# Sparse attention and a ReGLU feed-forward on one core: feed-forward banks, V products and attention pieces placed anew

## The chip, the cores and the metric

The kernel runs on one core of a Trainium2 chip. The metric is the device time of one execution in microseconds (us), the median of several runs. The engines are TensorE (PE, with its weight loads as PEld), VectorE (DVE), ScalarE (ACT), GpSimd (POOL) and SyncE (SP), which here issues DMAs only. Each engine works through its own instructions in the order in which the program has them.

## The reference

Two stages follow each other. The first is attention over q, k and v of shape (4, 8, 768, 64): 4 batches, 8 heads, 768 rows. A row sees the first 8 columns (global) and the 96 columns up to itself (local), with a bias that falls with the distance.

```python
scores = scale * np.matmul(q, k.transpose(0, 1, 3, 2))
keep = is_global | is_local
scores = scores + bias[None, :, :, :]          # -slope of the head * distance
scores = np.where(keep, scores, -1000000000.0)
a = np.exp(scores - max); a = a / sum(a)
attn = np.matmul(a, v)
```

The second is a feed-forward with a ReLU gate over x, the attention's output as 3072 rows of 512:

```python
gate = np.maximum(x @ w_gate, 0.0)             # 512 -> 1536
val = x @ w_val
out = gate * val @ w_out                       # 1536 -> 512
```

## The kernel before

The 3072 rows are worked in eight halves of 384 rows; half s is rows of batch s // 2. In the code they are counted from 0 (`s` in the attention, `c` in the feed-forward); this text counts them from one, so that half four is s = 3. The order of all work is written out by hand: a function that is called records its instructions on every engine at that place.

**Stages.** Stage one, on the PSUM pools `s` (two tiles of two banks) and `t` (four of one bank), does the attention of half one, a pair of heads p at a time, in small steps: `scores`, `masks`, `first_values` (V rows of the first half brought to their places by selector matmuls, then copied out of PSUM), `first_sums` (what = 0: sums of the weights; what = 1: product with V), `first_inverse` (Ln, then Exp of minus that, on ACT, into a tile `rc`) and `first_product` (DVE: product times inverse into `xT`, the feed-forward's input). Stage two, on pools `s`, `ff` and `t`, begins the feed-forward of half one (`begin`: for the first gate and the first val block, parts 0 to 2 of 4) and weaves it with the attention of half two. Pools take the eight PSUM banks in the order in which they are named; a tile waits for whoever used its bank in the stage before.

From the third stage on the pools are `ff` (3), `qk` (3) and `av` (2). `ffn_pieces(c)` gives the feed-forward of a half as items of about 0.65 us: 12 gate and 12 val blocks in turn (`gate` L518 with a ReLU on ACT, `val` L518 with a product `ht` on DVE), then output blocks. From half three on the output uses seven products of sums (L577), for which DVE makes `cb`, `ad` and `de` from `ht`; `behind` hangs these sums on val blocks 2, 5, 8, 9, 10 and 11. On val 11 hang three: ad, cb and de.

`attention_pieces(s)` gives the attention as a list of pieces: QK(p), three per head pair p (scores on PE L408, Exp on ACT L411, mask product on DVE L420), and AV(p), two per pair (product with V on PE L436, Ln on ACT L445; the second also the Exp L450 and two products into `xT` on DVE L453). Its end mixes pairs 2 and 3, where g is QK(3) and a is AV(2):

```python
return (QK(0) + QK(1) + AV(0) + QK(2) + AV(1) + g[0:1] + gap + a[0:1] + g[1:2] + a[1:2] + g[2:3]
        + gap + AV(3))
```

`spread(items, first, last)` puts the pieces at equal distances between two shares of the feed-forward's length, and `weave` records each piece behind the first item that reaches its share. While half c's feed-forward runs, the attention of half c + 1 is woven in. An empty piece (`gap`) takes a place and does nothing.

**Loads.** `early_pieces(s)` casts k and q on POOL (`kc`, `qz`), transposes them by DMA from SP's queue (`piece_xk` L376 into kN, `piece_xq` L380 into qT) and orders the keys on POOL (kT). Weights are loaded through POOL's queue; `wo_sb`, the output weights, is the last and largest, and a POOL instruction (`held`) waits for it before half three's last casts. Half four's q and k (`qs`, `ks`) are loaded behind half three's ordered keys. SP's queue carries in this order: three output stores of half one, half four's three kN transposes, another store, its three qT transposes, two more stores.

Of the kernel before, what the change touches and what calls it, by code (L numbers as in the profile page):

```python
# [8 lines left out]
FP32 = mybir.dt.float32  # L9
# [6 lines left out]
def kernel(  # L16
# [21 lines left out]
    HP = H // 2  # L38
    QH = S // 2
# [26 lines left out]
    rc_pool = ctx.enter_context(tc.tile_pool(name="rc", bufs=2))  # L66
# [6 lines left out]
    firstp = first.enter_context(tc.tile_pool(name="firstp", bufs=1, side="right"))  # L73
# [6 lines left out]
    def open_psum(**pools):  # L80
        stack = ExitStack()
        for name, bufs in pools.items():
            psum[name] = stack.enter_context(
                tc.tile_pool(name=name, bufs=bufs, space=PSUM, reuse_waits="tile"))
        return stack
# [35 lines left out]
    def v_dst(b, r0, r1, j):  # L121
        t = vbuf[b % 2][r0:r1, j, D:]
        return t.rearrange("p (h z) -> p h z", z=2 * D)[:, :, 0:D]
# [48 lines left out]

    v3 = firstp.tile([128, H, NN * D], BF16, name="v3")
    vb3 = firstp.tile([128, H, D], BF16, name="vb3")
    rc0 = [firstp.tile([128, QH], FP32, name=f"rc{p}") for p in range(3)]
    kq0 = firstp.tile([128, 2, H, NN * D], FP32, name="kq0")
    kq1 = setupp.tile([128, 2, H, NN * D], BF16, name="kq1")

# [131 lines left out]
    def first_values(j, copy):  # L310
        vt = psum["t"].tile([128, 512], FP32, name="t_ps")
        for n in range(NN):
            nc.tensor.matmul(vt, lhsT=sel[:, n, j, :], rhs=v3[:, :, n * D : (n + 1) * D],  # L313
                             start=(n == 0), stop=(n == NN - 1))
        copy(v_dst(0, 0, 128, j) if j < 3 else vb3, vt.rearrange("r (h d) -> r h d", d=D))
# [3 lines left out]
    def distances(p, g):  # L319
        ps = biased_of[p, g] = psum["s"].tile([128, 2, 512], FP32, name="s_ps")  # L320
        for e in range(2):
            c = 0
            for i, (j, a, w, m) in enumerate(by[0, j] for j in steps_of[0][g]):
                nc.tensor.matmul(ps[:, e, c : c + NN * w].rearrange("k (n t) -> k n t", n=NN),
                                 lhsT=diag[:, 2 * p + e],
                                 rhs=dd[:, 0 if j == 0 else 1, :, m : m + w],
                                 start=(i == 0), stop=False, skip_group_check=True)
                c += NN * w

    def scores(s, p, g):  # L330
        half = s % 2
        spans_ = [by[half, j] for j in steps_of[half][g]]
        biased = half == 0 and 2 * p < NB
        if biased and (p, g) not in biased_of:
            distances(p, g)
        ps = biased_of[p, g] if biased else psum["s"].tile([128, 2, 512], FP32, name="s_ps")
        es = ef_pool.tile([128, 2, 360], BF16, name=f"ef{g}")
        cols = sum(NN * w for _, _, w, _ in spans_)
        qd = qTb[s][:, p, 0, :].rearrange("d (n t) -> d n t", n=NN)
        c = 0  # L340
        for i, (j, a, w, m) in enumerate(spans_):
            for e in range(2):
                r = slice(64 * e, 64 * e + 64)
                nc.tensor.matmul(ps[:, e, c : c + NN * w].rearrange("k (n t) -> k n t", n=NN),  # L344
                                 lhsT=kT[0][p][r, j, :], rhs=qd[r, :, a : a + w],
                                 start=(i == 0 and not biased), stop=(i == len(spans_) - 1),
                                 skip_group_check=True)
            es_of[s, p, j] = (es, c)
            c += NN * w
        nc.scalar.activation(es[:, :, 0:cols], ps[:, :, 0:cols], AF.Exp, bias=0.0, scale=scale)  # L350
# [13 lines left out]
    def piece_cast_k(s, p):  # L364
        nc.gpsimd.tensor_copy(  # L365
            kc.rearrange("t n (h d) -> t h n d", d=D)[:, 2 * p : 2 * p + 2],
            ks_of[s][:, 2 * p : 2 * p + 2, :].rearrange("t e (n d) -> t e n d", n=NN))
# [7 lines left out]
    def piece_xk(s, n):  # L375
        nc.sync.dma_start_transpose(  # L376
            out=kNb[s % 2][:, :, n * 128 : (n + 1) * 128], in_=kc[:, n])
# [10 lines left out]
    def early_pieces(s):  # L388
        out = [(0.0, lambda p=p: piece_cast_k(s, p)) for p in range(HP)]
        out += [(0.0, lambda n=n: piece_xk(s, n)) for n in range(NN)]  # L390
        out += [(0.0, lambda p=p: piece_cast_q(s, p)) for p in range(HP)]
        out += [(0.0, lambda n=n: piece_xq(s, n)) for n in range(NN)]
        out += [(0.0, lambda p=p: piece_order(s, p)) for p in range(HP)]
        return out
# [61 lines left out]
    def first_sums(s, p, what, tile_=None):  # L456
        half = s % 2
        todo = [by[half, j] for g in steps_of[half] for j in g]
        av = psum["t"].tile([128, 512], FP32, name="t_ps") if tile_ is None else tile_[:, what]
        av3 = av[:, 0:QH].rearrange("d (n p) -> d n p", n=NN)  # L460
        for i, (j, a, w, m) in enumerate(todo):
            es, c = es_of[s, p, j]
            for e in range(2):
                z0 = D + 2 * D * (2 * p + e)
                vals = vb3[:, 2 * p + e] if (half, j) == (0, 3) else vbuf[0][:, j, z0 : z0 + D]
                nc.tensor.matmul(av3[64 * e : 64 * e + 64, :, a : a + w],
                                 lhsT=ones if what == 0 else vals,
                                 rhs=es[:, e, c : c + NN * w].rearrange("k (n p) -> k n p", n=NN),
                                 start=(i == 0), stop=(i == len(todo) - 1),
                                 skip_group_check=True)  # L470
        av_of[s, p, what] = av
# [6 lines left out]
    def first_inverse(s, p):  # L478
        ln = rc_pool.tile([128, QH], FP32, name="lnd")
        nc.scalar.activation(ln, av_of[s, p, 0][:, 0:QH], AF.Ln, bias=0.0, scale=1.0)  # L480
        rc = rc0[p % 3] if s == 0 else rc_pool.tile([128, QH], FP32, name="rcp")
        nc.scalar.activation(rc, ln, AF.Exp, bias=0.0, scale=-1.0)
        av_of[s, p, "r"] = rc

    def first_product(s, p):
        if s not in xT_of:
            xT_of[s] = xt_pool.tile([128, N_DC, QH], BF16, name="xT")
        nc.vector.tensor_tensor(xT_of[s][:, p, :], av_of[s, p, 1][:, 0:QH], av_of[s, p, "r"], op=ALU.mult)  # L488
# [2 lines left out]
        first_inverse(s, p)  # L491
        first_product(s, p)

    def attention_pieces(s):
        QK = lambda p: [(0.18, lambda g=g: piece_qk(s, p, g)) for g in range(3)]
        AV = lambda p: [(0.29, lambda e=e: piece_av(s, p, e)) for e in range(2)]
        g = QK(3)
        a = AV(2)
        gap = [(0.0, lambda: None)]
        return (QK(0) + QK(1) + AV(0) + QK(2) + AV(1) + g[0:1] + gap + a[0:1] + g[1:2] + a[1:2] + g[2:3]  # L500
                + gap + AV(3))

# [142 lines left out]
    def spread(items, first, last):  # L647

        n = len(items)
        return [(first + (i + 0.5) / n * (last - first), f) for i, (_, f) in enumerate(items)]  # L650
# [14 lines left out]
    V, A, P = nc.vector.tensor_copy, nc.scalar.copy, nc.gpsimd.tensor_copy  # L665
# [6 lines left out]
    stack = open_psum(s=2, t=4)  # L672
# [44 lines left out]
    first_keys(3, V)  # L717
    distances(2, 1)
    scores(0, 2, 0)
    first_values(0, V)  # L720
    scores(0, 2, 1)
    make_mask(5)
    first_values(1, V)
    scores(0, 3, 0)
    first_values(2, V)
    masks(0, 3, 0)
    scores(0, 3, 1)
    masks(0, 3, 1)
    first_values(3, A)
    spread_v_globals(0, 3, NT)  # L730
    first_sums(0, 2, 0)
    first_inverse(0, 2)
    first_sums(0, 0, 1)
    first_product(0, 0)
    first_sums(0, 3, 0)
    first_inverse(0, 3)
    for p in range(1, HP):
        first_sums(0, p, 1)
        first_product(0, p)
    stack.close()  # L740
# [3 lines left out]
    kc = pool.tile([128, NN, DM], BF16, name="kc")  # L744
    qz = pool.tile([128, NN, HP, 2, 128], BF16, name="qz")

    stack = open_psum(s=2, ff=2, t=2)
    f1_0, f2_0 = ffn_pieces(0)
    f1_1, f2_1 = ffn_pieces(1)
    g_of = [begin_of[0][1]] + [f for _, f in f1_0[2::2]]  # L750
# [57 lines left out]
    for f in (*cast_k[:3], *cast_q[:3], lambda: nc.gpsimd.tensor_copy(held, wo_sb[0:1, N_FC - 1, 0:1]),  # L808
# [4 lines left out]
    weave(f1_1[G[0]])  # L813
    weave(f1_1[G[1]], [(0.1 + 0.12 * j, lambda j=j: fill_ones(nc.vector, 0, j)) for j in range(NT)])
    weave(f1_0[G[2]] + f1_1[G[2]] + f2_0 + f2_1,
          spread(attention_pieces(2), 0.43, 0.92), spread(early_pieces(3), 0.6, 0.92),
          spread([(0.0, lambda name=name, part=part: wo_sum(name, part)) for name in late["bs"] for part in range(2)],
                 0.2, 0.8))

    for c in range(2, NHALF):  # L820
        placed = []
        if c + 1 < NHALF:
            placed.append(spread(attention_pieces(c + 1), 0.0, 0.78))
        if c + 2 < NHALF:
            load_qk(c + 2, 0, H)
            load_v_half(c + 2)
            placed.append(spread(early_pieces(c + 2), 0.25, 0.75))
        f1, f2 = ffn_pieces(c)
        weave(f1 + f2, *placed)
# [35 lines left out]
```

## Time and profile before

| What | Value |
|---|---|
| median of 3 runs | 244.82 us (244.53 to 245.05) |
| the profiled execution | 244.51 us |
| its span, first to last instruction | 242.6 us |
| granted TensorE clock | 1.000 |
| busy in the span | PE 97%, DVE 70%, ACT 63%, POOL 38% |
| DMA moved | 33.75 MB, 139 GB/s on the mean |

A row of the timeline gives the start in us from the span's start, the time it took, the engine, the line of the kernel, the operation, what it writes and reads, and how many instructions are in the row; in brackets, how long the engine was idle before it and what ended that. A row of the waits gives the engine, the line that waited, who ended the wait, and the total, number and longest of these waits in us. The chain of waits is followed back from the last instruction; its pieces have a start, a length and an engine, queue or DMA.

### The profile page before, as it was taken

To read this page: it belongs to the slowest core of one execution; us is meant where nothing else is said; L and a number is where in the kernel's file an instruction comes from. 1 tells how busy PE (TensorE), PEld (TensorE's weight loads), DVE (VectorE), ACT (ScalarE), POOL (GpSimd) and SP (SyncE) were. 2 spreads that over 40 slices of the span, in tenths; PEclk is the share of its full clock that TensorE was granted. 3 is DMA by queue.
4 is the path that set the end of the run, shared out by engine and by line. 5 is a ranking of instruction groups with operands and counts; after the bars stand their busy time and mean duration, and the time that the engine had idled before them with its cause. 6 is when DMAs were issued, how large, how long until landed. Compare 5 with 4: busy or idle time off the path is not lost.

```text
span 242.6 us, 5086 instructions
## 1 busy us (share of the span) xinstructions
PE 234.6 (97%) x1819; PEld 148.6 (61%) x1819; DVE 168.8 (70%) x442; ACT 152.3 (63%) x316; POOL 92.4 (38%) x233
## 2 busy tenths in 40 slices
PE   7899999999999899999999999999999999999994
PEld 3555555665554566586667666686667666685663
DVE  7775954756674478857796688858796678854643
ACT  5987883433885677647874687647874587634330
POOL 6866896119257436803555057302540000000000
PEclk9999999999999999999999999999999999999999
DMA  6999999997999999779459768829491200020003
GB/s 206 187 195 177 261 241 208 176 107 136 289 176 175 237 237 112 101 133 286 89 110 109 232 184 153 60 106 285 82 118 43 91 0 0 3 104 25 3 15 115
DMA packets 79392, 33.75 MB, mean 139 GB/s; under 512 B 56952, under 2 KB 76408, under 8 KB 79368
## 3 DMA queue, kind: packets, MB, share of 16 engines
q1 hardware_dynamic: 46408, 23.82, 41.7%
q0 software_dynamic: 31744, 8.71, 34.5%
q10 hardware_dynamic: 1216, 0.92, 1.2%
q8 instruction: 14, 0.23, 0.4%
q14 instruction: 10, 0.08, 0.1%
HBM read 28.41 MB, written 6.29 MB: 143 GB/s over the span
## 4 chain that ended last, share of the span: by engine, by line
PE 67%; DMA 19%; POOL 4%; DVE 3%; SPq 2%; ACT 2%; issue 1%; POOLq 0%
PE ff_ps L518 39%; PE ff_ps L577 8%; DMA wo_sb<-in_moe_w_out_dram 8%; PE ff_ps L538 6%; PE av_ps L436 5%; PE qk_ps L408 5%; DMA qs<-in_q_dram 4%; PE qk_ps L577 3%; DMA v<-in_v_dram 3%; DMA kN<-kc 2%; SPq L376 1%; DMA qT<-qz 1%; PE t_ps L313 1%; POOL kT L262 1%; POOL qz L373 1%
## 5 line engine op out<-in xcount | busy, mean ns | idle before, releaser
L518 PE MATMUL ff_ps<-xT,wv 128*128 128x384 bf16 x384 | 78.2, 326 | 0.6 <-DVE xT L488 0.6
L518 PE MATMUL ff_ps<-xT,wg 128*128 128x384 bf16 x384 | 78.2, 326 | 0.1
L525 ACT ACTIVATE grelu<-ff_ps 128x384 bf16<-128x384 f32 x96 | 46.8, 487 | 46.7 <-PE ff_ps L518 23.4
L531 DVE TENSOR_TENSOR ht<-ff_ps,grelu 128x384 bf16<-128x384 f32 x96 | 53.1, 554 | 20.8 <-PE ff_ps L518 16.0
L518 PEld LDWEIGHTS <-wv 128*128 128x128 bf16 x384 | 36.3, 97 | 23.1 <-issue 1.0
L518 PEld LDWEIGHTS <-wg 128*128 128x128 bf16 x384 | 35.6, 97 | 21.2
L420 DVE TENSOR_TENSOR es<-es,m_all 128x432 bf16<-128x432 bf16 (+5 forms) x108 | 32.9, 333 | 14.2 <-ACT es L411 12.8
L411 ACT ACTIVATE es<-qk_ps 128x432 bf16<-128x432 f32 (+2 forms) x72 | 37.2, 526 | 8.2 <-PE qk_ps L408 7.1
L453 DVE TENSOR_TENSOR xT<-av_ps,rcp 64x384 bf16<-64x384 f32 x48 | 26.6, 555 | 17.0 <-ACT rcp L450 16.0
L538 PE MATMUL ff_ps<-wo_sb,ht 128*128 128x512 bf16 x144 | 36.7, 379 | 0.0
L445 ACT ACTIVATE lnd<-av_ps 64x384 f32<-64x384 f32 x48 | 23.3, 485 | 15.8 <-PE av_ps L436 15.4
L365 POOL CAST kc<-ks 128x384 bf16<-128x384 f32 x24 | 11.7, 530 | 45.4 <-DMA ks<-in_k_dram 45.4
L408 PE MATMUL qk_ps<-qT,kT 128*128 128x432 bf16 (+5 forms) x108 | 25.0, 286 | 1.0 <-DMA qT<-qz 1.0
L436 PEld LDWEIGHTS <-vbuf 128*128 128x128 bf16 x216 | 18.2, 98 | 8.8 <-issue 0.9
L140 POOL DMA_DIRECT2D vbuf<-in_v_dram x25 | 21.6, 876 | 2.9 <-DMA wv<-in_moe_w_val_dram 1.6
L436 PE MATMUL av_ps<-es,vbuf 128*128 128x216 bf16 (+4 forms) x216 | 21.8, 226 | 0.7 <-DVE es L420 0.7
L538 PEld LDWEIGHTS <-ht 128*128 128x128 bf16 x144 | 13.0, 97 | 11.6 <-issue 0.3
L373 POOL CAST qz<-qs 128x192 bf16<-128x192 f32 x48 | 15.4, 367 | 6.5 <-issue 4.3
L408 PEld LDWEIGHTS <-kT 128*128 128x128 bf16 x108 | 10.5, 97 | 9.0 <-DMA qT<-qz 1.4
L450 ACT ACTIVATE rcp<-lnd 128x384 f32<-128x384 f32 x24 | 12.6, 523 | 0.8
L350 ACT ACTIVATE ef<-s_ps 128x720 bf16<-128x720 f32 (+2 forms) x16 | 11.1, 712 | 2.2 <-PE s_ps L344 2.0
L266 POOL COPY kT<-kN 128x240 bf16<-128x240 bf16 x16 | 6.8, 423 | 9.9 <-DMA kN<-kc 7.1
(112 smaller groups left out, 238.0 us busy)
## 6 DMA issues: line engine op xcount, KB each, us to landing
out_dram<-osb SPq DMA_DIRECT2D x22, 256.0 KB, 2.9
ks<-in_k_dram SPq DMA_DIRECT2D x6, 768.0 KB, 5.3
qs<-in_q_dram SPq DMA_DIRECT2D x6, 768.0 KB, 8.7
vbuf<-in_v_dram POOLq DMA_DIRECT2D x21, 120.0 KB, 8.8
wg<-in_moe_w_gate_dram POOLq DMA_DIRECT2D x3, 512.0 KB, 7.8
wv<-in_moe_w_val_dram POOLq DMA_DIRECT2D x3, 512.0 KB, 9.3
wo_sb<-in_moe_w_out_dram POOLq DMA_DIRECT2D x1, 1536.0 KB, 19.0
kq<-in_q_dram ACTq DMA_DIRECT2D x2, 192.0 KB
```

Of the source, the lines that this page charges most:

```text
L140: nc.gpsimd.dma_start(out=v_dst(b, NG + r0, NG + r0 + n, j), in_=v[b, :, KT * j + r0 : KT * j + r0 + n, :].rearrange("h p d -> p h d"))
L408: nc.tensor.matmul(ps[:, c : c + n_], lhsT=kt[:, j, :], rhs=qd[:, :, :, a : a + w], start=True, stop=True)
L411: nc.scalar.activation(es[:, 0:cols], ps[:, 0:cols], AF.Exp, bias=0.0, scale=scale)
L420: nc.vector.tensor_mul(e4, e4, mk)
L436: nc.tensor.matmul(av3[:, :, a : a + w], lhsT=vb[:, j, z0 : z0 + 128], rhs=es[:, c : c + NN * w].rearrange("k (n p) -> k n p", n=NN), star ...
L445: nc.scalar.activation(ln[o0 : o0 + 64], av[d0 : d0 + 64, 0:QH], AF.Ln, bias=0.0, scale=1.0)
L453: nc.vector.tensor_tensor(xT_of[s][r, p, :], av_of[s, p, e_][r, 0:QH], rc[r], op=ALU.mult)
L518: nc.tensor.matmul(st[key][:, 0:QH], lhsT=w_of(w, dc, fc), rhs=xT_of[c][:, dc, :], start=(dc == 0), stop=(dc == N_DC - 1))
L525: nc.scalar.activation(gr, psg[:, 0:QH], AF.Relu, bias=0.0, scale=1.0)
L531: nc.vector.tensor_tensor(ht[:, fc, :], psv[:, 0:QH], st["gr", fc], op=ALU.mult)
L538: nc.tensor.matmul(ps2, lhsT=ht[:, fc, n * 128 : (n + 1) * 128], rhs=wo_sb[:, fc, :], start=(fc == 0), stop=(fc == N_FC - 1))
L577: nc.tensor.matmul(st[key][:, 0:D2], lhsT=left(i), rhs=right(i), start=start and i == 0, stop=stop and i == N2 - 1, skip_group_check=not s ...
```

## The change

Five edits. (1) Stage two opens its pools in the order ff, s, t instead of s, ff, t: the feed-forward's two banks are now those that held scores tiles of stage one, and its score tiles take the banks in the middle. (2) In stage one scores(0, 2, 1) and scores(0, 3, 0) move ahead of first_values(0) and of the next steps; first_values(2) is copied out by ACT and first_values(3) by DVE, both behind the last masks. (3) first_sums(0, 0, 1) and first_product(0, 0) leave their place between the inverses and stand at the head of the loop over pairs; for that four `rc` tiles are kept instead of three. (4) Half three's attention gets two gaps instead of one ahead of AV(3), and its places end at 0.935 instead of 0.92. (5) Half four's attention (c = 2) begins at 0.06 of half three's feed-forward instead of 0.0; it still ends at 0.78.

```diff
-    rc0 = [firstp.tile([128, QH], FP32, name=f"rc{p}") for p in range(3)]
+    rc0 = [firstp.tile([128, QH], FP32, name=f"rc{p}") for p in range(HP)]
...
-        rc = rc0[p % 3] if s == 0 else rc_pool.tile([128, QH], FP32, name="rcp")
+        rc = rc0[p] if s == 0 else rc_pool.tile([128, QH], FP32, name="rcp")
...
-    def attention_pieces(s):
+    def attention_pieces(s, gaps=1):
...
-                + gap + AV(3))
+                + gaps * gap + AV(3))
...
     scores(0, 2, 0)
+    scores(0, 2, 1)
     first_values(0, V)
-    scores(0, 2, 1)
+    scores(0, 3, 0)
     make_mask(5)
     first_values(1, V)
-    scores(0, 3, 0)
-    first_values(2, V)
     masks(0, 3, 0)
     scores(0, 3, 1)
     masks(0, 3, 1)
-    first_values(3, A)
+    first_values(2, A)
+    first_values(3, V)
     spread_v_globals(0, 3, NT)
     first_sums(0, 2, 0)
     first_inverse(0, 2)
-    first_sums(0, 0, 1)
-    first_product(0, 0)
     first_sums(0, 3, 0)
     first_inverse(0, 3)
-    for p in range(1, HP):
+    for p in range(HP):
         first_sums(0, p, 1)
         first_product(0, p)
...
-    stack = open_psum(s=2, ff=2, t=2)
+    stack = open_psum(ff=2, s=2, t=2)
...
-          spread(attention_pieces(2), 0.43, 0.92), spread(early_pieces(3), 0.6, 0.92),
+          spread(attention_pieces(2, 2), 0.43, 0.935), spread(early_pieces(3), 0.6, 0.92),
...
-            placed.append(spread(attention_pieces(c + 1), 0.0, 0.78))
+            placed.append(spread(attention_pieces(c + 1), 0.06 if c == 2 else 0.0, 0.78))
```

In the changed program TensorE has the same instructions. Where half four's attention ends in half three's feed-forward, TensorE's order before was: val 10, a[1], gate 11, g[2], val 11, two output items, AV(3). Changed it is: val 10, gate 11, a[1], val 11, g[2], two output items, AV(3). VectorE's order there was: a[1]'s two xT products, g[2]'s mask, val 11's product, ad, cb, de. Changed it is: a[1]'s two xT products, val 11's product, ad, cb, de, g[2]'s mask.

## The prediction

> **What bounds the kernel now.** I read the page first, then TensorE's waits, then TensorE's timeline around each wait and the engine or queue that ended it.
>
> ```profile
> PE 234.6 (97%) x1819; PEld 148.6 (61%) x1819; DVE 168.8 (70%) x442; ACT 152.3 (63%) x316; POOL 92.4 (38%) x233
> ...
> PEclk9999999999999999999999999999999999999999
> ```
>
> TensorE (PE) is the bound, at full granted clock throughout, so time is won only where it waits. Its waits, by who ended them:
>
> ```profile
> PE qk_ps L408 <- DMA qT<-qz: 1.0, 1, 1.0
> PE av_ps L436 <- DVE es L420: 0.7, 2, 0.6
> PE ff_ps L518 <- DVE xT L488: 0.6, 1, 0.6
> ```
>
> From about 20 us on only three waits are left, at 74.5, 79 and 100.8 us. The change touches all three, and the start. The start, on PE's timeline:
>
> ```profile
> 18.95 0.49 PE L518 MATMUL ff_ps<-xT,wv 128*128 128x384 bf16 x2 [0.57 <-DVE xT L488]
> ...
> 20.02 0.86 PE L275 MATMUL t_ps<-ident,kq 128*64 128x128 bf16 x24
> ```
>
> The first val matmuls wait for the last product of the first half, because their bank is the one that this product reads. Six matmuls follow it, before the second half's transposes. The chain of waits, from 15 to 80 us, shows what stands at 79 us:
>
> ```profile
> 27.78 19.04 DMA wo_sb<-in_moe_w_out_dram
> ...
> 76.47 3.36 DMA qT<-qz
> ```
>
> A load that lands at 46.82 releases the casts and transposes of half three; those release the loads of half four, and their transposes end in qT at 79.84. SyncE's queue in the last stretch, back to back:
>
> ```profile
> 68.49 4.51 SPq L376 DMA_TRANSPOSE kN<-kc  x3
> ...
> 73.73 4.08 SPq L380 DMA_TRANSPOSE qT<-qz  x3
> ```
>
> The third wait, on PE's and on VectorE's (DVE) timeline:
>
> ```profile
> 98.29 0.35 PE L408 MATMUL qk_ps<-qT,kT 128*128 128x432 bf16 x1
> ...
> 100.42 0.37 PE L436 MATMUL av_ps<-es,vbuf 128*128 128x72 bf16 x4
> 100.95 0.25 PE L436 MATMUL av_ps<-es,vbuf 128*128 128x216 bf16 x1 [0.16 <-DVE es L420]
> ```
>
> ```profile
> 99.35 1.13 DVE L453 TENSOR_TENSOR xT<-av_ps,rcp 64x384 bf16<-64x384 f32 x2
> 100.51 0.38 DVE L420 TENSOR_TENSOR es<-es,m_all 128x432 bf16<-128x432 bf16 x1
> 100.93 0.56 DVE L531 TENSOR_TENSOR ht<-ff_ps,grelu 128x384 bf16<-128x384 f32 x1
> 101.52 0.36 DVE L565 TENSOR_TENSOR ad<-ht 128x384 bf16<-128x384 bf16 x1
> 101.80 0.55 DVE L561 TENSOR_TENSOR cb<-ht 128x768 bf16<-128x768 bf16 x1
> 102.27 0.35 DVE L570 TENSOR_TENSOR de<-ht 128x384 bf16<-128x384 bf16 x1
> ```
>
> The mask that PE waits for ends at 100.90; val 11's product and three operand sums come after it. The change reverses just that order.
>
> **The start.** With the feed-forward banks on the bank pair of scores(0, 3, 0), whose Exp began at 14.13 and took 0.77, only data holds the first matmuls. Gate and val blocks 0 to 2 run while the products run; after the last product come two matmuls instead of six: 4 x 0.163 = 0.65 us (the chain has 0.65 us for each four). The reordering moves one score group (0.25 us) into PE's 0.44 us wait for v at 11.6. The V copy on ScalarE (ACT) no longer stands between the scores and the Ln; ACT's chain Ln, Exp, Ln, Exp should end near 17.9 instead of 18.31. Against that, the V copy of DVE (0.69) now precedes all four products, since each reads vb3. With V ending on PE near 15.5, masks done, copy done at 16.3, products at about 0.5 us each: the last ends near 18.7 instead of 18.90. PE reaches the transposes near 19.1, but their q load was issued at 9.71 and needs 9.5 us: 19.2. So PE gains about 0.8 us here; 0.4 if a copy or mask slips, 0.9 at best. The fourth rc tile costs nothing, and POOL's added wait on ACT in a much later V load is long over.
>
> **What is kept of it.** Little. The DMA share (overlapping packets count twice) is 1.1 to 2.4 in every 2 us stretch from 20 to 50 us, and the software queue has always another load behind, so issuing the 26 us loads 0.8 us earlier should not land wo_sb earlier. Half three's qT lands at 58.30 in the trace's records; its first score matmul started at 58.70, and one needs 0.13 us after landing (79.84 to 79.97). PE therefore keeps 58.70 - 58.43 = 0.27 us and waits for the rest.
>
> **Half three's last A·V.** It stood at 74.12, and its third matmul started at 75.05, 0.75 us later than the 0.09 us steps of the first two would have it. One gap more puts it one item (three output matmuls, 0.65 us) later; a[0] moves an item earlier, so ACT takes its Ln ahead of the output copy and the mask ends some 0.3 us earlier. The 0.75 us go. Both Lns now follow each other, so the fourth gate matmul of half three's feed-forward waits about 0.3 us for xT.
>
> **Half four's start, the intended gain.** At 0.06 its first score piece stands behind gate 0, val 0 and gate 1, before behind gate 0 alone: two items of four matmuls, 8 x 0.163 = 1.30 us of work done ahead of the wait. Gate 0's last matmul started at 78.62 and was through at 78.78, so PE would come to the scores at 78.78 - 0.27 - 0.75 + 0.3 + 1.30 = 79.36, some 0.6 us ahead of the old start at 79.97. How early may qT be? SyncE's transposes start right behind the third output store, which waits for PE and ACT; PE is 0.27 us earlier there, so they may be. But the first took 1.89 us to issue, where the later halves' first takes 1.20 to 1.23, and half four's q load landed only at 68.71; if that load held it, nothing moves. So between 79.70 and 79.97; I take 79.85. Gain: 1.30 + 0.12 = 1.42 us.
>
> **Half four's end, the price.** With 22 pieces over 0.06 to 0.78 of 35 items, a[1] of head pair 2 moves one item later, g[2] of pair 3 too, and A·V of pair 3 stays (item 26). In the changed program's order g[2]'s mask stands on DVE behind val 11's product and ad, cb and de. On the old clock, PE coming to A·V at 100.42 both times: a[1] ends 0.65 us later on PE (98.47); ACT takes relu 11 first (to 98.65), then Ln 0.49 and Exp 0.52, to 99.69; two xT products, 1.14, to 100.86; the product and the sums, from 100.93 to 102.62 in the trace, 1.69 us of which 0.08 overlaps, to 102.47; the mask, 0.38 with 0.08 overlap, to 102.77. PE's fifth A·V matmul goes at 102.82 instead of 100.95: 1.87 us more, 1.6 to 2.1. Queued behind it are the remaining output matmuls, all seven product blocks and half four's gates; nothing on PE can pass it. DVE has slack after, so the loss is not given back.
>
> Bounds below nothing for this wait: it would vanish only if relu, Ln, Exp and the sums were done 1.9 us sooner, and all of them start from PE's own a[1].
>
> At this place a rule bears against the change. The wait of 1.03 us at 79 left PEclk at 9; the new one is about 2.2 us long. The Trainium skill, "TensorE: Matmul & The Clock Gate", section "Why this matters for your kernels", warns of PE idle gaps over some 3 us, after which the clock halves. By that page this gap stays under it; if it crossed, an estimate from its window of 3.4 us at half clock would be 1.7 us more.
>
> **Sum.** -1.42 + 1.87 = +0.45 us on the profiled execution's 244.51 us (span 242.6 and 1.9 around it), so 244.96. The median of the runs is 244.82, 0.31 above that execution: 245.2. About 0.2% (0.49 us) is what a measurement of this kernel tells from no change, so this forecast lies just inside it on the slow side; by itself it covers 244.9 to 245.6.
>
> **Rivals.**
>
> *The transfers follow PE.* If wo_sb or the SyncE transposes do come earlier by what PE gained, the scores start at PE's arrival, 79.2 to 79.4, and the gain is 1.9 to 2.05 us: the change is even to 0.2 us faster, 244.6. For it: SyncE is back to back behind a store that PE releases. Against it: the full DMA shares, and the slow first issue. It decides from a start before 79.40; faster by over 0.2% needs 78.9.
>
> *The transfers come later.* Stores and V loads of half five fall into the last transposes' time; if qT lands 0.4 us later, the loss is 0.9 us: 245.7. Against it: the order on SyncE is the same.
>
> *The mask is not late.* If the late mask doesn't show, because DVE reaches it no later than PE needs it, the wait at A·V stays 0.3 us and the change is 1.4 us faster: 243.4. Against it: the order of DVE's instructions in the built program, which is fixed.
>
> *The start gains nothing.* If DVE's copy holds up the products, all 0.8 us go; as only 0.27 is kept, the time is 0.1 to 0.3 us longer than forecast, 245.4. I count it with the forecast.
>
> **How the numbers follow.** Forecast 0.58 (of it 0.32 over the 0.2%, 0.26 inside), transfers follow 0.18 (0.04 faster, 0.14 inside), transfers later 0.14, mask not late 0.10. So faster 0.14, same 0.40, slower 0.46. The range takes in both transfer cases with the 0.25 us of the wait's own bounds, 244.3 to 245.9; the last rival is left out.
>
> **What would show it.** Right: the val wait at 18.4 gone, a new PE wait of 0.3 to 0.6 us for qT near 58, none at 74, the qT wait still there but behind gate 1, and a wait of about 2.2 us for DVE's mask in the fifth matmul of an A·V near 100 us, with ad, cb and de just ahead of the mask. Wrong: that wait under 1 us; or half four's first scores before 79.4 us.

## The result, and the profile after

The changed kernel takes 246.34 us (median of 5 runs, 245.54 to 246.66), the kernel before, measured beside it, 244.53 us (243.98 to 245.05). The ratio is 1.0071 (95% interval 1.0044 to 1.0097). The forecast was 245.2 with a range up to 245.9: slower was right, the size too small. The profiled execution took 246.34 us with a span of 244.2 us, against 242.6 before: 1.6 us to explain.

The busy row and the granted clock of the page of the changed kernel:

```profile
PE 234.6 (96%) x1810; PEld 149.1 (61%) x1819; DVE 168.3 (69%) x442; ACT 152.1 (62%) x316; POOL 92.7 (38%) x233
...
PEclk9999999999999999999999999999999999999999
```

TensorE's work is the same 234.6 us at full clock (some matmul records are missing). So the loss is waiting, and TensorE's waits name it:

```profile
PE av_ps L436 <- DVE es L420: 1.9, 1, 1.9
...
PE qk_ps L408 <- POOL ks L169: 0.8, 1, 0.8
PE ff_ps L538 <- DVE ht L531: 0.5, 1, 0.5
...
PE av_ps L436 <- DVE xT L453: 0.2, 1, 0.2
```

The start, on TensorE's timeline, in which the whole begin blocks now run without a wait and the transposes start at 19.14 instead of 20.02:

```profile
18.72 0.33 PE L518 MATMUL ff_ps<-xT,wg 128*128 128x384 bf16 x1
18.88 0.33 PE L518 MATMUL ff_ps<-xT,wv 128*128 128x384 bf16 x1
19.14 0.93 PE L275 MATMUL t_ps<-ident,kq 128*64 128x128 bf16 x24
```

Half three's scores, where those 0.88 us end, on TensorE's timeline before and after: 58.94, later than the 58.70 of before. The wait is put down to the last POOL instruction ahead of them (L169), but that one had ended at 58.62. By the trace's records the last of half three's qT landed at 58.85 (58.30 before), so the wait is for qT:

```profile
58.70 0.35 PE L408 MATMUL qk_ps<-qT,kT 128*128 128x432 bf16 x1
...
58.94 0.34 PE L408 MATMUL qk_ps<-qT,kT 128*128 128x432 bf16 x1 [0.76 <-POOL ks L169]
```

The chain of waits of the changed kernel has `wo_sb`, landed at 47.72 (46.82 before), ahead of half three's last casts and transposes, and qT, landed at 80.24 (79.84 before), ahead of half four's scores.

```profile
26.96 20.76 DMA wo_sb<-in_moe_w_out_dram
...
76.90 3.34 DMA qT<-qz
```

Half four's scores on TensorE's timeline, before and after: now behind gate 0, val 0 and gate 1, they start at 80.37 instead of 79.97. That is 0.40 later with 1.30 us more work done: TensorE is 0.90 us ahead of its old self. The waits list no wait for qT there any more; TensorE and qT arrive at nearly the same time.

```profile
79.97 0.37 PE L408 MATMUL qk_ps<-qT,kT 128*128 128x144 bf16 x2 [1.03 <-DMA qT<-qz]
...
79.41 0.81 PE L518 MATMUL ff_ps<-xT,wg 128*128 128x384 bf16 x4
80.37 0.36 PE L408 MATMUL qk_ps<-qT,kT 128*128 128x144 bf16 x2
```

The end of half four's attention on TensorE's timeline. The fifth A·V matmul starts at 102.56; before it was 100.95, so the lead of 0.90 is now a lag of 1.61, and nothing later changes that.

```profile
98.15 0.35 PE L408 MATMUL qk_ps<-qT,kT 128*128 128x432 bf16 x1
99.01 1.46 PE L538 MATMUL ff_ps<-wo_sb,ht 128*128 128x512 bf16 x5 [0.52 <-DVE ht L531]
100.31 0.37 PE L436 MATMUL av_ps<-es,vbuf 128*128 128x72 bf16 x4
102.56 0.25 PE L436 MATMUL av_ps<-es,vbuf 128*128 128x216 bf16 x1 [1.88 <-DVE es L420]
```

VectorE's timeline there has the mask last, as the order of the program has it:

```profile
94.06 1.14 DVE L453 TENSOR_TENSOR xT<-av_ps,rcp 64x384 bf16<-64x384 f32 x2 [1.05 <-ACT rcp L450]
...
99.36 1.13 DVE L453 TENSOR_TENSOR xT<-av_ps,rcp 64x384 bf16<-64x384 f32 x2
100.52 0.56 DVE L531 TENSOR_TENSOR ht<-ff_ps,grelu 128x384 bf16<-128x384 f32 x1
101.11 0.36 DVE L565 TENSOR_TENSOR ad<-ht 128x384 bf16<-128x384 bf16 x1
101.39 0.55 DVE L561 TENSOR_TENSOR cb<-ht 128x768 bf16<-128x768 bf16 x1
101.86 0.35 DVE L570 TENSOR_TENSOR de<-ht 128x384 bf16<-128x384 bf16 x1
102.13 0.37 DVE L420 TENSOR_TENSOR es<-es,m_all 128x432 bf16<-128x432 bf16 x1
```

From 94.06, where the xT products of the pair before start, to the mask no row has a bracket: VectorE does not idle there (in the kernel before this stretch begins at 93.98). The Exp on ScalarE that a[1]'s xT products need had ended at 98.95, 0.41 us before they started:

```profile
98.43 0.52 ACT L450 ACTIVATE rcp<-lnd 128x384 f32<-128x384 f32 x1
```

### The profile page after: what moved, and what is told of

Read it like the earlier page. It is cut to its first block, busy times and chain, and to the rows that moved or that the text cites. A ratio compares the mean times of both kernels' runs of the same rounds, so it can differ in the third digit from the quotient of the medians.

```text
span 244.2 us, 5074 instructions
## 1 busy us (share of the span) xinstructions
PE 234.6 (96%) x1810; PEld 149.1 (61%) x1819; DVE 168.3 (69%) x442; ACT 152.1 (62%) x316; POOL 92.7 (38%) x233
## 4 chain that ended last, share of the span: by engine, by line
PE 67%; DMA 17%; POOL 4%; DVE 4%; ACT 3%; SPq 2%; issue 1%; POOLq 0%
PE ff_ps L518 38%; DMA wo_sb<-in_moe_w_out_dram 9%; PE ff_ps L577 8%; PE ff_ps L538 6%; PE av_ps L436 5%; PE qk_ps L408 4%; DMA qs<-in_q_dram 4%; PE qk_ps L577 3%; DMA kN<-kc 2%; SPq L376 2%; DMA qT<-qz 1%; DMA kq<-in_k_dram 1%; PE t_ps L275 1%; ACT ef L350 1%; POOL kT L262 1%
## 5 line engine op out<-in xcount | busy, mean ns | idle before, releaser
L420 DVE TENSOR_TENSOR es<-es,m_all 128x432 bf16<-128x432 bf16 (+5 forms) x108 | 32.4, 329 | 13.8 <-ACT es L411 12.7
L453 DVE TENSOR_TENSOR xT<-av_ps,rcp 64x384 bf16<-64x384 f32 x48 | 26.7, 555 | 19.2 <-ACT rcp L450 18.2
L538 PE MATMUL ff_ps<-wo_sb,ht 128*128 128x512 bf16 x135 | 35.9, 378 | 1.0 <-DVE ht L531 0.5
L140 POOL DMA_DIRECT2D vbuf<-in_v_dram x25 | 21.6, 877 | 2.5 <-DMA wv<-in_moe_w_val_dram 2.2
```

The source lines that it names most:

```text
L140: nc.gpsimd.dma_start(out=v_dst(b, NG + r0, NG + r0 + n, j), in_=v[b, :, KT * j + r0 : KT * j + r0 + n, :].rearrange("h p d -> p h d"))
L420: nc.vector.tensor_mul(e4, e4, mk)
L453: nc.vector.tensor_tensor(xT_of[s][r, p, :], av_of[s, p, e_][r, 0:QH], rc[r], op=ALU.mult)
L538: nc.tensor.matmul(ps2, lhsT=ht[:, fc, n * 128 : (n + 1) * 128], rhs=wo_sb[:, fc, :], start=(fc == 0), stop=(fc == N_FC - 1))
```

## The experiments

All ratios are to the kernel before, run on the same chip beside them (244.35 to 244.68 us).

### Which edit costs the time

**The changed kernel with edit 5 undone:**

```diff
-            placed.append(spread(attention_pieces(c + 1), 0.06 if c == 2 else 0.0, 0.78))
+            placed.append(spread(attention_pieces(c + 1), 0.0, 0.78))
```

> The changed kernel with edit 5 undone (half four's attention from 0.0 again). Theory late mask: the loss is VectorE's order at the end of half four's attention, so with the old places the A.V wait near 100 us falls from 2.0 to about 0.3 us, the output block's wait for a bank goes, and the time is 1.2 to 1.8 us under the changed kernel: 244.4 to 245.0, within 0.4 us of before. Rival late loads: the loss is wo_sb landing 0.9 us later because the start issues its loads earlier; that stays, half four's first scores stay near 80.4 us with less work ahead of them, and the time is still 0.4 us or more above before.

244.76 us, ratio 1.0014 (0.9996 to 1.0032). The loss is gone: TensorE waits 1.44 us for qT at 79 and none at the end (all five A·V matmuls in one row, from 100.45).

**The kernel before with edit 5 alone** (the same line the other way round):

> The kernel before with edit 5 alone (half four's attention from 0.06). Theory late mask: half four's first scores start at about 80.1 us with 1.30 us more work done, a gain of 1.2 us; the A.V wait near 100 us grows by 1.7 us and the output block may wait 0.5 us for a bank, so the time is 0.5 to 1.0 us over before. Rival late loads: nothing at the start is changed, wo_sb lands near 46.8 us, and the kernel is faster than before by up to 1.2 us.

245.89 us, ratio 1.0067 (1.0041 to 1.0094). Edit 5 alone is as slow as the whole change, by the same wait (the first two rows). What the rival expected of `wo_sb`, a landing near 46.8, did not come: with the start of the kernel before it landed at 48.54 (the last row, from the chain of waits), and half three's scores waited 0.79 us, until 59.16.

```profile
100.56 0.37 PE L436 MATMUL av_ps<-es,vbuf 128*128 128x72 bf16 x4
102.64 0.25 PE L436 MATMUL av_ps<-es,vbuf 128*128 128x216 bf16 x1 [1.71 <-DVE es L420]
...
27.29 21.25 DMA wo_sb<-in_moe_w_out_dram
```

**The kernel before with edits 1 to 3** (the earlier start alone):

> The kernel before with edits 1 to 3 alone (banks, order of stage one). Theory late mask: the second half's transposes start near 19.1 instead of 20.0 us, and all but 0.3 us of it is waited away at half three's first scores and at half four's; the time is within 0.3 us of before. Rival late loads: wo_sb lands 0.5 to 0.9 us later than 46.8 us, half three's first scores start near 58.9, half four's near 80.4, and the time is 0.4 us or more over before.

245.11 us, ratio 1.0022 (0.9997 to 1.0048): no gain. The transposes started at 19.06, but the later ones waited 0.61 us for the q load until 20.03; `wo_sb` landed at 49.23, and half three's scores waited 1.07 us until 59.91. One of the twelve executions took 857.2 us; it is not in the ratio, and no trace of it was kept.

**The kernel before with edit 4** (the second gap alone):

> The kernel before with the second gap ahead of half three's last A.V alone (and its spread to 0.935). Theory (PE's waits are in series with qT of half four): the wait of 0.6 us at 74 goes, but PE then stands that much longer at qT near 79, so the time stays within 0.2% of the kernel before: 244.2 to 244.6, with a qT wait of 1.3 to 1.7 us. Rival (qT follows PE, by SyncE's stores): the scores of half four start near 79.4 and the time is 243.8 or less.

244.37 us, ratio 0.9992 (0.9981 to 1.0003). The wait at 74 is gone, and TensorE stands 1.22 us at qT instead of about 1.0: the two waits are in series, and removing the first only lengthens the second.

### Is it VectorE's order, or the places of the pieces?

**The changed kernel with val 11's three sums behind the first output item** (half three only):

```diff
-            for f in behind.get(fc, ()):
+            for f in behind.get(fc, ()) if c != 2 or fc < N_FC - 1 else ():
...
+        if c == 2:
+            f2[0] = (0.65, out_and_sums)      # first output item, then the three sums
```

> The changed kernel with val block 11's three sums (ad, cb, de) of half three moved on VectorE behind the first output item, so behind the last mask. Theory late mask: the mask comes 1.1 to 1.3 us sooner, TensorE's wait at A.V falls from 2.0 to 0.8 us, and the time is 1.0 to 1.3 us under the changed kernel. Rival late loads: the same time as the changed kernel within 0.3 us, since the loads are as they were.

244.41 us, ratio 1.0004 (0.9984 to 1.0024). With the mask right behind the product (100.09 instead of 102.13) TensorE waits 0.57 us instead of 1.88, and edit 5 itself is untouched. That is 1.31 of the 1.9 us by which the median fell. In the profiled execution half four's scores also started 0.56 us earlier (79.81), with `wo_sb` landed at 47.21, which the moved sums do not explain.

**The changed kernel with the three sums computed twice:**

```diff
-            for f in behind.get(fc, ()):
+            for f in behind.get(fc, ()) * (2 if c == 2 and fc == N_FC - 1 else 1):
```

> The changed kernel, with the three operand sums behind half four's val 11 in half three's feed-forward computed a second time, ahead of the same mask. Theory (the mask stands behind the sums on DVE, and DVE is never idle there): the steps from ad to cb, de and the mask were 0.28, 0.47 and 0.27 us, so PE's wait in the fifth A.V matmul grows from 1.88 us by 1.0 to 1.9..3.1 us in all, near 2.9, and the kernel by as much: 247.1 to 247.4, about 1.011 to 1.012 of the kernel before. Rival (the wait is set by the chain relu, Ln, Exp on ACT or by the val product): the wait stays near 1.9 us and the time near 246.2.

246.82 us, ratio 1.0097 (1.0067 to 1.0127). The mask starts 3.77 us after a[1]'s xT products (99.12 to 102.89) instead of 2.77, just the 1.0 us of the added sums. TensorE's wait grew by 0.83 us:

```profile
103.32 0.25 PE L436 MATMUL av_ps<-es,vbuf 128*128 128x216 bf16 x1 [2.71 <-DVE es L420]
```

The wait follows what stands ahead of the mask; the chain of Ln and Exp does not set it. The median rose by 0.5 us and the profiled execution by 0.70, less than the 1.0 expected. The profile has a part of the reason: the wait ahead of the output items was 0.21 there instead of 0.52.

**The changed kernel with all of half four's pieces at their old places, the first two held until 0.06:**

```diff
-            placed.append(spread(attention_pieces(c + 1), 0.06 if c == 2 else 0.0, 0.78))
+            pieces = spread(attention_pieces(c + 1), 0.0, 0.78)
+            placed.append([(max(t, 0.06), f) for t, f in pieces] if c == 2 else pieces)
```

> The changed kernel with half four's pieces back at their old places (0.0 to 0.78), except that the first two wait until 0.06: the same head, the old end. Theory late mask: the loss sits in the order at the end, so the A.V wait near 100 us falls to 0.3 us, the output block waits for nothing, the 1.3 us of the head are kept: 1.8 to 2.5 us under the changed kernel and 0.4 to 1.2 us under before. Rival DVE bound: VectorE has too little idle time in half three's feed-forward to follow a TensorE that is 1.3 us further on, whatever the order; the wait stays over 1 us, spread over the same two places, and the time is that of before within 0.3 us.

243.52 us, ratio 0.9957 (0.9938 to 0.9975): faster than both kernels. Half four's scores start at 80.36, as in the changed kernel (80.37), so the two differ only in what comes behind. The fifth A·V matmul is 2.51 us earlier, at 100.05 (TensorE's timeline of this run):

```profile
99.50 0.37 PE L436 MATMUL av_ps<-es,vbuf 128*128 128x72 bf16 x4
100.05 0.25 PE L436 MATMUL av_ps<-es,vbuf 128*128 128x216 bf16 x1 [0.17 <-DVE es L420]
```

VectorE's timeline of this run shows both parts of these 2.51 us:

```profile
93.07 1.14 DVE L453 TENSOR_TENSOR xT<-av_ps,rcp 64x384 bf16<-64x384 f32 x2 [0.74 <-ACT rcp L450]
...
98.45 1.13 DVE L453 TENSOR_TENSOR xT<-av_ps,rcp 64x384 bf16<-64x384 f32 x2
99.61 0.38 DVE L420 TENSOR_TENSOR es<-es,m_all 128x432 bf16<-128x432 bf16 x1
```

a[1]'s xT products start at 98.45, against 99.36 in the changed kernel: 0.91 us. The mask follows them at once, 1.16 us after their start, against 2.77 (99.36 to 102.13): 1.61 us for product and sums.

**The kernel before with the same hold alone:**

> The kernel before with that head alone (the first two pieces of half four's attention wait until 0.06, all others stay). Theory late mask: 0.9 to 1.2 us faster than before, nearly all of the wait of 1.0 us for qT being filled. Rival DVE bound: within 0.3 us of before.

243.12 us, ratio 0.9956 (0.9942 to 0.9971). The hold without edits 1 to 4 gains as much, a little more than expected. TensorE has no wait for qT at 79 any more.

**The kernel before with the second gap, the first three pieces held until 0.12:**

```diff
+            placed.append([(max(t, 0.12), f) for t, f in pieces] if c == 2 else pieces)
```

> The kernel before with edit 4 (two gaps, 0.935) and the first three pieces of half four's attention held until 0.12, four items of work ahead of them instead of one... five items in all. Theory late mask: the 0.75 us wait at 74 us goes and is no longer paid at qT, since more work stands ahead of it; 1.3 to 1.9 us faster than before. Rival DVE bound: within 0.4 us of before, the gain at the head given back near 100 us.

243.55 us, ratio 0.9971 (0.9948 to 0.9995). Half four's scores start at 80.97 with no wait ahead, but TensorE then waits 0.45 us for an Exp at 81.7. Once TensorE is the bound at the head, waiting longer with the first piece buys nothing. The gain of 0.9 us lies between what the theory (1.3 to 1.9) and the rival (0.4 at most) expected.

### Where the start's gain goes

**The kernel before, profiled once more:**

> The kernel before, profiled a second time. If wo_sb's landing moves by itself from run to run, it lands between 46.5 and 48.6 us and half four's first scores move with it by up to 1 us; if it lands at 46.8 within 0.2 us again, the later landings of the edited kernels are their own doing.

244.2 us, span 242.3; `wo_sb` landed at 46.90 (46.82 in the first), half four's scores started at 79.69 (79.97).

**The changed kernel without the POOL copy that waits for `wo_sb`:**

```diff
-    for f in (*cast_k[:3], *cast_q[:3], lambda: nc.gpsimd.tensor_copy(held, wo_sb[0:1, N_FC - 1, 0:1]),
+    for f in (*cast_k[:3], *cast_q[:3],
```

> The changed kernel without the one-element copy that makes POOL wait for wo_sb ahead of half three's last casts; nothing else differs. Theory (the start's gain is lost because half three's qT waits for wo_sb's landing): the casts end near 44 instead of 48.9, qT of half three lands near 55, PE's wait of 0.76 us at 58 goes, and half three's scores start near 58.2. What follows at 80 us depends on SyncE's transposes of half four, which stand behind the third output store: if they come earlier with PE, 0.7 us are kept (245.4 to 245.7); if their loads hold them, PE waits as much longer for qT near 79.5 and the time stays at 246.0 to 246.4. Rival (something else than wo_sb holds the scores at 58.9): they stay at 58.9 and so does the time.

245.33 us, ratio 1.0039 (1.0021 to 1.0058), about 1.0 us under the changed kernel. Half three's scores start at 57.91, and all that follows is as much earlier, SyncE's transposes too (67.70 instead of 68.73), so that half four's scores start at 79.34 instead of 80.37. The intervals of the two ratios overlap a little, so the traces carry this reading. SyncE's timeline of the changed kernel and of this run, then TensorE's of this run:

```profile
68.73 4.71 SPq L376 DMA_TRANSPOSE kN<-kc  x3
...
67.70 4.20 SPq L376 DMA_TRANSPOSE kN<-kc  x3
72.00 0.52 SPq L544 DMA_DIRECT2D out_dram<-osb  x1
72.63 4.06 SPq L380 DMA_TRANSPOSE qT<-qz  x3
```

```profile
57.91 0.35 PE L408 MATMUL qk_ps<-qT,kT 128*128 128x432 bf16 x1
...
79.34 0.36 PE L408 MATMUL qk_ps<-qT,kT 128*128 128x144 bf16 x2
```

**Two more without that copy.** Edits 1 to 4 with the hold in place of edit 5:

> The changed kernel with pieces from 0.0 to 0.78, the first two held until 0.06, and without the copy that waits for wo_sb. Theory (the start's gain of 0.8 us is real and is lost only because half three's q and k wait for wo_sb; SyncE's transposes of half four follow PE): half three's scores start near 57.9 and half four's near 79.3, against 58.96 and 80.36 with the copy, and the time is 0.7 to 1.0 us under the 243.5 us with it: 242.5 to 242.8. Rival (the landing varies by itself and the copy costs nothing): 243.3 to 243.7.

242.61 us, ratio 0.9928 (0.9914 to 0.9942), 0.9 us under the same kernel with the copy, and the fastest of all runs here. Its waits have no row for half three's or half four's scores, and none for the last mask: all five A·V matmuls stand in one row.

```profile
97.22 1.46 PE L538 MATMUL ff_ps<-wo_sb,ht 128*128 128x512 bf16 x6
98.52 0.63 PE L436 MATMUL av_ps<-es,vbuf 128*128 128x72 bf16 x5
```

The kernel before with the hold:

> The kernel before with the first two pieces held until 0.06, and without the copy that waits for wo_sb. With the copy the scores of half three already started at 58.10 and those of half four at 79.56, both without a wait for qT. Theory (PE is the bound there, so an earlier qT buys nothing without the earlier start): 243.0 to 243.3, no change from 243.1. Rival (the copy costs the start whatever comes ahead): 242.4 or less.

243.11 us, ratio 0.9952 (0.9937 to 0.9966), with the copy 243.12. So the copy is worth nothing with the old start and 0.9 us with the new one. This is the start's gain: real, but held back where half three's q and k wait for `wo_sb`.

### What a still longer wait costs

**The changed kernel with the three sums computed three times:**

> As the run before, with the three sums computed three times in all. Theory: PE's wait near 3.9 us, 2.0 more than in the changed kernel, time 248.1 to 248.4, ratio about 1.016, with the granted clock of the slices behind it at 9 (tenths). The Trainium skill, "TensorE: Matmul & The Clock Gate", section "Why this matters for your kernels", warns of idle gaps over some 3 us: by it the clock would halve behind this wait, with an estimate of 1.7 us more (about 250), and PEclk of the slice behind 103 us well under 9. Rival (wait not set by the sums): near 246.2.

The profiled execution behaved by the theory: 247.24 us, clock 1.0, wait 3.73 us.

```profile
103.52 0.25 PE L436 MATMUL av_ps<-es,vbuf 128*128 128x216 bf16 x1 [3.73 <-DVE es L420]
```

But the four executions took 247.24, 247.35, 250.78 and 251.01 us, the last two at a mean granted clock of 0.986. The ratio, 1.0166 (1.0089 to 1.0243), mixes the two levels. **The same kernel again:**

> The run with the three sums computed three times, once more. Its wait of 3.73 us left the granted clock at 1.0 in the profiled execution, but two other executions took 250.8 and 251.0 us at a mean clock of 0.986. Theory (a PE idle gap of 3.7 us is near the edge of the clock gate and crosses it in some executions): again two groups of times, near 247.3 at clock 1.0 and near 250.9 at 0.986, 3.5 us apart, and nothing between. Rival (those two were disturbed by something else): all near 247.3.

Six executions: four of 249.2 to 249.7 us at a clock of 0.993, two of 250.2 and 251.5 at 0.986; ratio 1.0214 (1.0199 to 1.0230). So there are three levels, not the two expected, and this kernel, whose wait is 3.73 us in both profiles, had a lower clock in 8 of 10 executions. The profiled one shows where. In stretches of its span, the columns are the length, busy time and number of instructions of PE, PEld, DVE, ACT and POOL, then the granted clock, the DMA share and GB/s:

```profile
102.00:104.00 2.00, 0.00 (x0) 0.00 (x0) 2.00 (x7) 0.00 (x0) 0.75 (x2) 0.90 1.49 94
104.00:106.00 2.00, 0.78 (x3) 0.40 (x3) 1.17 (x4) 0.41 (x1) 0.00 (x0) 0.50 0.84 53
106.00:108.00 2.00, 2.00 (x9) 0.97 (x8) 0.00 (x0) 0.59 (x3) 0.00 (x0) 0.50 0.00 0
108.00:110.00 2.00, 2.00 (x10) 1.19 (x9) 1.11 (x2) 1.08 (x2) 0.00 (x0) 0.50 0.00 0
110.00:112.00 2.00, 2.00 (x18) 1.70 (x17) 0.00 (x0) 1.12 (x3) 0.00 (x0) 0.89 0.34 131
```

The wait lasts from 101.49 to 105.22. By the shares of the rows the clock falls to half at about 103.6, 2.1 us into the wait, and stays there until about 110.4, some 6.8 us in all. That is a mean of 0.986 over the span; 0.993 would be about half as long. From the end of the wait to half four's first gate block TensorE needs 8.81 us (105.22 to 114.03); in the execution at full clock it needed 6.28 (103.52 to 109.80). The lower clock cost 2.53 us there. In the run with the sums twice, a wait of 2.71 us, all four executions kept 0.999 or more. The Trainium skill, "TensorE: Matmul & The Clock Gate", section "Why this matters for your kernels", puts the edge at some 3 us, which agrees with these two waits. An estimate from that page's window of 3.4 us would be 1.7 us at half clock; the measured cost was higher.

## Why the prediction was wrong, step by step

**Right in kind.** The val wait at 18.4 gone, no wait of 0.6 at 74 (0.2 is left at 70), a new wait near 58, half four's scores behind gate 1, and the late mask in the fifth A·V matmul near 100, with ad, cb and de ahead of it: all are in the trace (the wait near 58 was 0.76 us, over the 0.6 named; the wait for qT behind gate 1 is not listed). So is the sign. Two terms of the sum were mis-sized, both in the same direction. (The last addition, 244.96 + 0.31, gives 245.27, put down as 245.2; this changes nothing.)

**The end: 1.87 predicted, 2.51 measured.** The run with the hold has TensorE at half four's scores at the same time as the changed kernel (80.36 and 80.37), so it is the fair zero: 102.56 - 100.05 = 2.51. The product and the three sums ahead of the mask were sized right (1.69 less 0.08, that is 1.61, and 1.61 measured), but the mask behind them then has the overlap of 0.08 taken off once more: some 0.1 us of the miss. The rest, 0.54, is the step in front of them, which failed: "a[1] ends 0.65 us later on PE (98.47); ACT takes relu 11 first (...) to 99.69; two xT products". This follows one piece on one chain and finds the xT products starting 0.37 us later than in the trace of before (99.72 against 99.35). They started 0.91 us later than with the hold (98.45 and 99.36). From 94 us on VectorE is never idle, so their start is set by VectorE's queue, not by a[1]'s Exp, which had ended by 98.95, 0.41 us before they started. And that queue's start had moved: its stretch begins with the xT products of the pair before, at 94.06 against 93.07 with the hold, because edit 5 moved those pieces to later items too.

Counted on TensorE, the assumption that failed is "PE coming to A·V at 100.42 both times". The wait in front of the mask grew by 1.71 us (0.17 to 1.88), even less than the 1.87 predicted, but TensorE came to these A·V matmuls 0.81 us later (100.31 against 99.50 with the hold). Of that 0.52 is the wait ahead of the output items, which the prediction did not have; the same queue explains it, since the product that frees their bank was as late as the rest.

**The head: 1.42 predicted, 0.90 measured.** The 1.30 us for two items were right. The step that failed is "between 79.70 and 79.97; I take 79.85": the scores started at 80.37. The prediction kept 0.27 us of the start's gain, with `wo_sb` landing as before, and let SyncE's transposes come earlier by about half of that. In the profiled execution nothing was kept: `wo_sb` landed 0.90 us later, the scores of half three started 0.24 us later, SyncE's first kN transpose as well (68.73 against 68.49); that one took 2.08 us to issue instead of 1.89, and qT landed 0.40 us later.

The bound from half four's q load, which the prediction allowed for, did not show, though the chain of waits passes through that load. In the run with the hold POOL's casts behind this load began at 68.39 instead of 69.20, and the transposes (68.75 and 68.73) and half four's scores (80.36 and 80.37) came at the same time all the same. What the transposes follow is TensorE: in all 17 profiles the first of them starts 9.78 to 9.80 us after half three's first scores (57.91 to 59.91).

This miss is not shown to be the change's doing; a part of it is bad luck with `wo_sb`. The kernel with the sums three times has the same start and the same edit 5. In its first profile `wo_sb` landed at 46.73, half three's scores started at 57.99 and half four's at 79.48, a gain of 1.79 us, more than the 1.42 predicted.

**The sum.** -0.90 + 2.51 = +1.61 us, the 1.6 us by which the spans differ.

**The rivals.** *The mask is not late* is refuted by the wait. *The transfers come later* named the size at the head, 0.4 us, but another cause (stores and V loads); with the prediction's own price for the end it would still have given too little. *The transfers follow PE* was refuted as an account of this change, yet its mechanism is what the run without the copy shows: SyncE's transposes follow TensorE through the output stores, one for one. The full DMA shares, one argument against it, bear on `wo_sb` only. *The start gains nothing* is wrong at 19 us (0.88 gained) and right from 58 us on in the profiled execution.

**The clock.** The prediction said that the wait would stay under the edge of the clock gate. It did: 1.88 us, clock 1.0.

**Open.** Why `wo_sb` lands when it does was not settled. In the two profiles of the kernel before it landed at 46.82 and 46.90, in the two of the kernel with the sums three times at 46.73 and 49.10. With edit 5 alone, which leaves the order of everything ahead of 78 us as it was, it landed at 48.54. So a landing 0.90 us later needs no edit; whether the earlier start adds to it was not separated. Nor is it shown why, with the sums computed twice, the median rose by only 0.5 us when the wait grew by 0.83.

## What to carry to other kernels

Moving a whole list of pieces to clear a wait at its head moves its tail as well: hold back only the pieces that wait (here a maximum instead of a new start) and leave the others where they were. When a piece goes later, price it on every engine that takes part, by that engine's own queue: find where its last idle time ended and ask what starts that stretch, instead of following one chain through it. A gain at the start is worth what the next fixed landing lets through, so look for what waits for that landing, and whether it must.

## What the runs showed of the hardware

A wait of TensorE of 3.73 us came with a lower clock in 8 of 10 executions, so that it cost more than its length: in the lowered execution that was profiled, the granted clock went to half 2.1 us into the wait and stayed there until some 5 us after it, at a cost of 2.5 us. With 2.71 us that did not happen in 4 executions. The length of the wait alone does not decide: the other profiled execution had the same 3.73 us and kept the full clock. One execution of six with edit 5 alone, whose longest wait from 20 us on was 1.71 us in its profile, and one of twelve with edit 5 undone (1.44 us) also had a mean clock of 0.993; they have no trace, and their cause is not known.

The same load in the same program varies: `wo_sb` was issued between 26.7 and 28.5 us and landed 19.0 to 21.6 us later in all profiles here. So a difference of 1 us in what waits for it need not be the effect of an edit.
